# Hedgehog attention with a gated feed-forward: the product of the query exponentials with the key sums goes from VectorE to GpSimd

## The chip, the cores and the metric

The kernel runs on one core of one Trainium2 chip. The metric is device time in microseconds of that core, from runs of the whole program. A profiled execution, taken with the hardware profiler, shows what each engine did: TensorE does the matrix products (PE, with its weight loads as PEld), VectorE (DVE) and ScalarE (ACT) the element-wise work, GpSimd (POOL) element-wise work between buffers of the on-chip memory SBUF, and SyncE (SP) issues transfers. Only TensorE writes the accumulation memory PSUM in this kernel's products; VectorE and ScalarE read it.

## The reference

For 2048 rows of 576 features the reference computes a linear attention with a learned feature map, times a gate made by a feed-forward network, on the layer-normed input `xn`:

```python
pq = einsum("bhsd,hdf->bhsf", q, w_phi)          # 32 heads of 18
pk = einsum("bhsd,hdf->bhsf", k, w_phi)
phi_q = concat([softmax(pq), softmax(-pq)], -1)
phi_k = concat([softmax(pk), softmax(-pk)], -1)
kv  = einsum("bhsf,bhsd->bhfd", phi_k, v)
z   = einsum("bhsf->bhf", phi_k)
num = einsum("bhqf,bhfd->bhqd", phi_q, kv)
den = einsum("bhqf,bhf->bhq", phi_q, z)[..., None] + 1e-6
s   = (num / den) reshaped @ wo
g   = silu((silu(xn @ w_gate) * (xn @ w_up)) @ w_down)
out = x + s * g
```

What matters here is `den`: for each query row and head the 36 features are multiplied with the sums `z` over all keys, and added up.

## The kernel before

The program runs through four stages: layer norm with the transposed input and the folded weights; a key stage, which accumulates `kv` and `z`; a query stage, from about 218 to 457 us of the profiled execution; and the feed-forward, which fills the rest. Float32 products are made of three products of high and low parts, so TensorE has far more work than the plain sizes say.

The query stage handles sixteen tiles of 128 rows, two to a pair, in eight pairs. For a tile, `q_tile` makes the logits in the PSUM tile `p2` (28 products; there is one buffer of `p2`, so the next tile's logits have to wait until VectorE has read these), then `softmax_parts` takes maxima and minima (`m`, L530), subtracts them (`e`, L531, two halves), has ScalarE take the exponentials (L534, two halves) and VectorE add them up per head (`sm`, L538). Then come the lines around the change: `ez` is the product of the exponentials with `zb`, which holds the key sums `z` on all 128 partitions (L832); `y` is the sum of `ez` per head (L834); six small operations make the factor of each head (L836 to L841); and L842 multiplies the exponentials with it, `e<-e,y`. `numer` transposes the finished `e` of both tiles of a pair (`pt`, L854), splits them in high and low parts (`ph` by ScalarE L73, `pl` by VectorE L74), multiplies with `kv` (L861) and splits the result (`oh`, `ol`); `project` multiplies with `wo` (`p`, L889, 56 products). In program order the numerator of one pair comes ahead of the logits of the next.

Three other pieces of work run inside this stage. Early feed-forward tiles (`early_tile`, products `pe` at L108) need nothing of the attention and fill TensorE where it would wait. `tails` prepares pieces of the feed-forward weights: SP loads `tl` (L808), GpSimd makes four differences (L810 to L813), ScalarE and VectorE split them (`th` L815, `tl` L816), and GpSimd issues twelve transfers to `t_dram` (L819). `split_wo` splits `wo` in the first pair.

The order on each engine is fixed when the program is built. A planner in the language's library goes through all instructions, takes on each engine the one that comes first in program order among those that it holds to be ready, with its own estimate of how long each takes, and writes one list per engine; `issue_after` and `high_priority` shift a few places. On the chip every engine works through its list strictly in order, and waits at an instruction whose inputs are not there. So a filler product stands where the planner expected a gap, and what the planner estimated wrongly becomes a wait on the chip.

Of the kernel before, what the change touches and what calls it, by code (L numbers as in the profile page):

```python
# [52 lines left out]
def heads(ap):  # L53
    return ap.rearrange("p (h d) -> p h d", d=DH)


def spread(ap, n):
    return ap.unsqueeze(2).to_broadcast([P, n, DH])
# [3 lines left out]
def gated_hedgehog_kernel(ctx: ExitStack, tc, x, w_qk, w_v, consts_in, wo, w_gu, w_tail, w_down, out):  # L62
# [5 lines left out]
    nc = tc.nc  # L68
# [26 lines left out]
    def block(t):  # L95
        return t // HT, (t % HT) // 4, slice((t % 4) * P, (t % 4 + 1) * P)

    def xw(ps, i, j, cols, wh, wl, stationary_x):
        pairs = []
        for k in range(2):  # L100
            b = XB[i][2 * j + k]
            for c in range(2):
                pairs += [(b[:, c, cols], w[:, k, c]) for w in (wh, wl)]
                pairs += [(b[:, 3 + c, cols], wh[:, k, c])]
            pairs += [(b[:, 2, cols], wh[:, k, 2])]
        for n, (a, b) in enumerate(pairs):
            l, r = (a, b) if stationary_x else (b, a)
            last = nc.tensor.matmul(ps, l, r, start=n == 0, stop=n == len(pairs) - 1)  # L108
        return last
# [46 lines left out]
    with ExitStack() as att:  # L156
# [18 lines left out]
        with ExitStack() as wst:  # L175
# [349 lines left out]
            def softmax_parts(ps, e):  # L525
                m = kk_pool.tile([P, 2, H], F32, name="m", bufs=1)
                p4 = ps[:, :, 0:HALF].rearrange("p a (h d) -> p a h d", d=DH)
                for s, op in enumerate((ALU.max, ALU.min)):
                    m3 = m[:, s].rearrange("p (a h) -> p a h", a=2)
                    nc.vector.tensor_reduce(m3, p4, axis=AX.X, op=op)  # L530
                    read.append(nc.vector.tensor_sub(e[:, s * D:(s + 1) * D].rearrange("p (a h d) -> p a h d", a=2, d=DH),  # L531
                                                     p4, m3.unsqueeze(3).to_broadcast([P, 2, H // 2, DH])))
                for s in range(2):
                    last = nc.scalar.activation(e[:, s * D:(s + 1) * D], e[:, s * D:(s + 1) * D], AF.Exp,  # L534
                                                scale=1.0 if s == 0 else -1.0)
                exps.append(last)
                sm = kk_pool.tile([P, 2 * H], F32, name="sm")
                nc.vector.reduce_sum(sm, heads(e), axis=AX.X)  # L538
                return sm
# [206 lines left out]
        with ExitStack():  # L746
# [3 lines left out]
            zb = qc.tile([P, 2 * D], F32, name="zb")  # L750
# [33 lines left out]
        with ExitStack() as qst:  # L784
# [38 lines left out]
            def q_tile(t):  # L823
                i0, j0, cols = block(t)
                pq = qps.tile([P, 2, 512], F32, name="p2")
                for i in range(2):
                    w = slice(i * HALF, (i + 1) * HALF)
                    xw(pq[:, i, 0:HALF], i0, j0, cols, QH[:, :, :, w], QL[:, :, :, w], True)
                e = qk.tile([P, 2 * D], F32, name="e", bufs=4)
                r = softmax_parts(pq, e).rearrange("p (s h) -> p s h", s=2)  # L830
                ez = qk.tile([P, 2 * D], F32, name="ez", bufs=1)
                nc.vector.tensor_mul(ez, e, zb)  # L832
                y = qk.tile([P, 2 * H], F32, name="y")
                nc.vector.reduce_sum(y, heads(ez), axis=AX.X)  # L834
                y2 = y.rearrange("p (s h) -> p s h", s=2)
                nc.vector.scalar_tensor_tensor(y2[:, 0], r[:, 0], DEN_EPS, y2[:, 0], op0=ALU.mult, op1=ALU.add)  # L836
                nc.vector.tensor_mul(y2, y2, r[:, ::-1])
                den = qk.tile([P, H], F32, name="den")
                nc.vector.tensor_add(den, y2[:, 0], y2[:, 1])
                nc.vector.reciprocal(den, den)  # L840
                nc.vector.tensor_mul(y2, r[:, ::-1], den.unsqueeze(1).to_broadcast([P, 2, H]))  # L841
                last_e.append(nc.vector.tensor_mul(heads(e), heads(e), spread(y, 2 * H)))  # L842
                return e
# [56 lines left out]
            for n in range(S // QS + 1):  # L900
                new = []
                if n > 0:
                    om = numer(es)
                if n < S // QS:
                    new += [q_tile(order[n] * (QS // P) + j) for j in range(QS // P)]
                if n == 0:
                    split_wo()
                if n > 0:
                    project(order[n - 1], *om, n == S // QS)
                es = new  # L910
# [646 lines left out]
```

## Time and profile before

| | |
|---|---|
| median of three runs | 1579.47 us (1579.38 to 1579.89) |
| the profiled execution: its time | 1580.98 us |
| its span, first to last instruction | 1579.2 us |
| TensorE busy | 1570.4 us (99%) |
| VectorE busy | 1162.8 us (74%) |
| GpSimd busy | 671.5 us (43%) |
| granted TensorE clock | 1.00 |

The profiled execution took 1.5 us more than the median of the runs, and 1.8 us of its time lie outside the span. Sums over the trace are made against the span; a difference found there carries over to the time. Shares over the whole span mix stages with different limits: in the query stage VectorE is busy for 16 to 20 us of each 20 us, far above its mean.

### The profile page before, as it was taken

Reading aid. Unit: us, or ns where it says so; the run is one execution under the profiler, and the core shown is the slowest. Engines: PE = TensorE matmul, PEld = TensorE weight load, DVE = VectorE, ACT = ScalarE, POOL = GpSimd, SP = SyncE. Lnnn points to the kernel's source line nnn. Section 1 sums busy time; section 2 is a strip of 40 time slices with the busy share of each in tenths; the row PEclk is TensorE's granted clock in tenths of the full one; section 3 lists DMA queues with packets and bytes.
Section 4 is the critical chain, followed back from the end, with each engine's and each line's share of the span. In section 5 each row is a group of like instructions: output and inputs, shape, how many; then the busy total and the mean of one; then the engine's idle time right before and its main releaser. Section 6 shows DMA issues by size and latency. Waiting matters only on the chain.

```text
span 1579.2 us, 25305 instructions
## 1 busy us (share of the span) xinstructions
PE 1570.4 (99%) x9371; PEld 1415.5 (90%) x9371; DVE 1162.8 (74%) x1722; ACT 729.0 (46%) x1408; POOL 671.5 (43%) x723
## 2 busy tenths in 40 slices
PE   9999999999999999999999999999999999999998
PEld 7999999999988898898888888888888888888887
DVE  7777769999947787987777778545766667666577
ACT  6633344545445644444544444454333343333334
POOL 5766653334125545563644444313323324133133
PEclk9999999999999999999999999999999999999999
DMA  9424343336357455454545543964545655555445
GB/s 284 142 67 165 135 154 117 105 118 209 120 185 259 159 181 198 161 182 174 186 161 202 177 168 125 355 210 139 155 146 157 193 173 161 175 184 187 145 118 182
DMA packets 123287, 269.05 MB, mean 170 GB/s; under 512 B 12436, under 2 KB 54100, under 8 KB 121884
## 3 DMA queue, kind: packets, MB, share of 16 engines
q1 hardware_dynamic: 110572, 246.57, 47.6%
q0 software_dynamic: 3552, 12.59, 2.8%
q10 hardware_dynamic: 9040, 8.28, 1.6%
q8 instruction: 74, 1.21, 0.3%
q14 instruction: 49, 0.40, 0.1%
HBM read 167.54 MB, written 99.09 MB: 169 GB/s over the span
## 4 chain that ended last, share of the span: by engine, by line
PE 96%; POOL 1%; DVE 1%; DMA 1%; issue 1%; ACT 0%; SPq 0%; DVEq 0%; POOLq 0%; ACTq 0%
PE px L1014 25%; PE pd L1136 25%; PE pw L1014 12%; PE p L108 6%; PE py L1014 6%; PE pe L108 5%; PE p L889 4%; PE kvp L547 2%; PE pt L861 2%; PE pe L50 1%; PE vx L636 1%; PE pt L854 1%; PE tp L50 1%; PE vw L636 1%; DMA wst<-in_A_w_qk 0%
## 5 line engine op out<-in xcount | busy, mean ns | idle before, releaser
L1136 PEld LDWEIGHTS pd<-dw,hh 128*128 128x128 f32 x3000 | 421.8, 188 | 19.8 <-DVE acc L1372 0.8
L1136 PE MATMUL pd<-dw,hh 128*128 128x288 f32 x3000 | 435.7, 294 | 0.0
L1014 PE MATMUL px<-X,w 128*128 128x512 f32 x1512 | 385.6, 390 | 0.0
L1014 PEld LDWEIGHTS px<-X,w 128*128 128x128 f32 x1512 | 274.6, 188 | 46.1
L1014 PE MATMUL pw<-X,w 128*128 128x512 f32 x744 | 188.8, 389 | 0.0
L1014 PEld LDWEIGHTS pw<-X,w 128*128 128x128 f32 x744 | 139.5, 188 | 28.9
L1372 DVE TENSOR_TENSOR acc<-pd,acc 128x576 f32<-128x576 f32 x128 | 96.4, 753 | 93.3 <-PE pd L1136 92.6
L1047 DVE TENSOR_TENSOR s<-pw,s 128x512 f32<-128x512 f32 x126 | 86.4, 687 | 89.5 <-ACT s L1042 78.9
L1042 ACT COPY s<-px 128x512 f32<-128x512 f32 x126 | 73.6, 584 | 144.9 <-PE px L1014 144.7
L73 ACT CAST hh<-ha 128x512 fp32r<-128x512 f32 x139 | 82.2, 620 | 94.2 <-PE pd L1136 68.7
L74 DVE TENSOR_TENSOR hh<-ha,hh 128x512 fp32r<-128x512 f32 x139 | 111.8, 829 | 18.8 <-ACT hh L73 18.5
L1344 POOL TENSOR_TENSOR hb<-hb 128x512 f32<-128x512 f32 x34 | 46.6, 1372 | 157.2 <-DVE hb L1059 156.8
L74 DVE TENSOR_TENSOR w<-ld,w 128x512 fp32r<-128x512 f32 (+1 forms) x96 | 76.9, 803 | 38.6 <-ACT w L73 37.7
L1014 PE MATMUL px<-X,wt 128*128 128x512 f32 x252 | 98.0, 389 | 0.0
L1014 PE MATMUL py<-X,w 128*128 128x512 f32 x378 | 96.5, 390 | 0.0
L1357 POOL TENSOR_TENSOR ha<-ha 128x512 f32<-128x512 f32 x34 | 52.3, 1554 | 100.1 <-DVE hh L74 94.7
L1331 POOL TENSOR_TENSOR h<-ha,hb 128x512 f32<-128x512 f32 x34 | 44.5, 1309 | 107.2 <-DVE ha L1063 76.4
L983 POOL TENSOR_TENSOR ts<-ld 128x256 f32<-128x256 f32 x32 | 26.8, 839 | 139.6 <-issue 67.4
L73 ACT CAST w<-ld 128x512 fp32r<-128x512 f32 (+1 forms) x96 | 52.7, 550 | 70.3 <-POOL ld L986 40.6
L1067 ACT COPY py<-px 128x512 f32<-128x512 f32 x63 | 36.0, 572 | 106.1 <-PE px L1014 94.6
L108 PE MATMUL pe<-X,wh 128*128 128x512 f32 x260 | 80.4, 395 | 0.0
L1014 PEld LDWEIGHTS py<-X,w 128*128 128x128 f32 x378 | 68.3, 188 | 10.8
(325 smaller groups left out, 3242.3 us busy)
## 6 DMA issues: line engine op xcount, KB each, us to landing
w_dram<-w SPq DMA_DIRECT2D x90, 512.0 KB, 2.6
w<-w_dram SPq DMA_DIRECT2D x90, 512.0 KB, 4.3
wt<-t_dram SPq DMA_DIRECT2D x62, 336.0 KB, 4.4
ld<-in_B_w_gu SPq DMA_DIRECT2D x32, 512.0 KB, 6.3
rt<-in_B_w_down SPq DMA_DIRECT2D x33, 288.0 KB, 5.1
rb<-in_B_w_down SPq DMA_DIRECT2D x33, 288.0 KB, 3.3
w_dram<-w SPq DMA_DIRECT2D x30, 256.0 KB, 2.1
w<-w_dram SPq DMA_DIRECT2D x30, 256.0 KB, 2.7
```

The costliest lines, as they stand in the source:

```text
L73: cast = nc.scalar.copy(hi, src)
L74: return cast, nc.vector.tensor_sub(lo, src, hi)
L108: last = nc.tensor.matmul(ps, l, r, start=n == 0, stop=n == len(pairs) - 1)
L889: nc.tensor.matmul(ps[:, 0:HALF], a, bw, start=k == 0, stop=k == len(mm) - 1)
L1014: nc.tensor.matmul(ps, l, r, start=first and n == 0, stop=last and n == len(mm) - 1, skip_group_check=True)
L1042: snaps.append(nc.scalar.copy(t, ps))
L1047: nc.vector.tensor_add(t, ps, t)
L1136: nc.tensor.matmul(ps, l, r, start=first and n == 0 and m == 0, stop=n == len(hs) - 1 and m == 2, skip_group_check=True)
L1331: sub(s, g["h"][0][0], g["h"][0][1])
L1344: nc.gpsimd.tensor_add(a21, a21, g["h"][1][1])
L1357: sub(a12, a12, g["h"][0][0])
L1372: adds.append(nc.vector.tensor_add(a2, pd[:, :, 0:HALF], a2))
```

## The change

In `q_tile`, the product of the exponentials with the key sums is issued to GpSimd instead of VectorE. Nothing else in the source differs:

```diff
                 e = qk.tile([P, 2 * D], F32, name="e", bufs=4)
                 r = softmax_parts(pq, e).rearrange("p (s h) -> p s h", s=2)
                 ez = qk.tile([P, 2 * D], F32, name="ez", bufs=1)
-                nc.vector.tensor_mul(ez, e, zb)
+                nc.gpsimd.tensor_mul(ez, e, zb)
                 y = qk.tile([P, 2 * H], F32, name="y")
                 nc.vector.reduce_sum(y, heads(ez), axis=AX.X)
```

The planner makes a new order from it. The instructions are the same apart from the sixteen that change engine, and the lists of all engines agree up to the query stage and, but for a few transfers and differences at its end, from the feed-forward on. In between they differ at three places that matter here.

GpSimd, at the start of the query stage, behind the last split of the key stage's sums (`slo`). Before:

```order
L580 TENSOR_TENSOR slo<-sraw,shi 128x512
L810 TENSOR_TENSOR tl<-tl 128x128
L811 TENSOR_TENSOR tl<-tl 128x128
L812 TENSOR_TENSOR tl<-tl 128x128
L813 TENSOR_TENSOR tl<-tl 128x128
L810 TENSOR_TENSOR tl<-tl 128x128
```

and with the change:

```order
L580 TENSOR_TENSOR slo<-sraw,shi 128x512
L810 TENSOR_TENSOR tl<-tl 128x128
L832 TENSOR_TENSOR ez<-e,zb 128x1152
L811 TENSOR_TENSOR tl<-tl 128x128
L812 TENSOR_TENSOR tl<-tl 128x128
L810 TENSOR_TENSOR tl<-tl 128x128
L813 TENSOR_TENSOR tl<-tl 128x128
```

The first tile's `ez` stands behind the first difference of the tail weights, L810, which needs the load of `tl`.

VectorE, the first tile and the logits of the second (`p_2505`). Before:

```order
L538 TENSOR_REDUCE sm<-e 128x64
L832 TENSOR_TENSOR ez<-e,zb 128x1152
L530 TENSOR_REDUCE m<-p_2505 128x32
L834 TENSOR_REDUCE y<-ez 128x64
L531 TENSOR_TENSOR e<-p_2505,m 128x576
L836 SCALAR_TENSOR_TENSOR y<-sm,y 128x32
L530 TENSOR_REDUCE m<-p_2505 128x32
L837 TENSOR_TENSOR y<-y,sm 128x64
L531 TENSOR_TENSOR e<-p_2505,m 128x576
```

and with the change:

```order
L538 TENSOR_REDUCE sm<-e 128x64
L834 TENSOR_REDUCE y<-ez 128x64
L530 TENSOR_REDUCE m<-p_2505 128x32
L836 SCALAR_TENSOR_TENSOR y<-sm,y 128x32
L531 TENSOR_TENSOR e<-p_2505,m 128x576
L837 TENSOR_TENSOR y<-y,sm 128x64
L530 TENSOR_REDUCE m<-p_2505 128x32
L839 TENSOR_TENSOR den<-y 128x32
L531 TENSOR_TENSOR e<-p_2505,m 128x576
```

`y` now stands directly behind `sm`, ahead of all reading of the second tile's logits.

VectorE, the fourth tile (its last read of the logits stands some rows ahead). Before:

```order
L531 TENSOR_TENSOR e<-p_2704,m 128x576
L816 TENSOR_TENSOR tl<-tl,th 128x896
L538 TENSOR_REDUCE sm<-e 128x64
L832 TENSOR_TENSOR ez<-e,zb 128x1152
L834 TENSOR_REDUCE y<-ez 128x64
L836 SCALAR_TENSOR_TENSOR y<-sm,y 128x32
```

and with the change:

```order
L842 TENSOR_TENSOR e<-e,y 128x1152
L74 TENSOR_TENSOR ol<-pt,oh 126x256
L538 TENSOR_REDUCE sm<-e 128x64
L834 TENSOR_REDUCE y<-ez 128x64
L816 TENSOR_TENSOR tl<-tl,th 128x896
L836 SCALAR_TENSOR_TENSOR y<-sm,y 128x32
```

Here too `y` follows `sm` at once, and L816, the low part of the first tail weights, stands behind it. Over the sixteen tiles `y` stands directly behind `sm` in ten; in the other six, one or two short operations lie between. On TensorE the filler products between the starts of the first and the seventh pair's projections go from 169 to 108, and stand behind the last projection instead.

## The prediction

> **What bounds the kernel now.** I read the page's busy times and its chain of waits first, then the busy times in stretches of the query stage, then the groups of that stage, then single instructions around two of its tiles.
>
> ```profile
> PE 1570.4 (99%) x9371; PEld 1415.5 (90%) x9371; DVE 1162.8 (74%) x1722; ACT 729.0 (46%) x1408; POOL 671.5 (43%) x723
> PE 96%; POOL 1%; DVE 1%; DMA 1%; issue 1%; ACT 0%; SPq 0%; DVEq 0%; POOLq 0%; ACTq 0%
> ...
> 240.00:260.00 20.00, 20.00 (x112) 17.28 (x111) 19.91 (x32) 10.81 (x17) 2.41 (x6) 1.00 0.38 120
> 280.00:300.00 20.00, 20.00 (x149) 19.47 (x149) 18.89 (x31) 10.11 (x19) 5.69 (x13) 1.00 0.31 86
> 360.00:380.00 20.00, 20.00 (x144) 18.97 (x142) 19.29 (x31) 10.61 (x19) 6.48 (x13) 1.00 0.76 251
> ...
> 456.98 10.89 PE pe L108 x48
> ```
>
> TensorE is busy 99% of the span, and the chain that ended last runs through it for 96%. In the query stage (the stretches from 240 on; the columns are PE, PEld, DVE, ACT, POOL) it is never idle, but VectorE stands at 19 to 20 of 20 us beside it: here two engines are at their limit, and the fillers `pe` are what keeps TensorE full. One filler product costs 10.89/48 = 0.227 us. The number of products does not change, so the time can only change by what TensorE waits. It waits for next to nothing now, so there is next to nothing to gain.
>
> How tightly the two are coupled shows at the sixth tile, in the order of time:
>
> ```profile
> 301.08 1.52 DVE L842 TENSOR_TENSOR e<-e,y 128x1152 f32<-128x1152 f32 x1
> ...
> 302.27 0.40 PE L108 MATMUL pe<-X,wh 128*128 128x512 f32 x1
> 302.65 0.85 PE L854 MATMUL pt<-consts,e 128*72 128x128 f32 x6
> ```
>
> L842 ends at 302.60, and the transposes start 0.05 us later: the planner placed as many fillers as VectorE's chain took, to within one product. If that chain is later on the chip than the planner thinks, TensorE stands still for all of the difference.
>
> **What moves, and its price.** From the groups of the query stage, and of GpSimd over the whole span:
>
> ```profile
> L842 DVE TENSOR_TENSOR e<-e,y 128x1152 f32<-128x1152 f32 x16 | 22.0, 1374 | 0.4
> L832 DVE TENSOR_TENSOR ez<-e,zb 128x1152 f32<-128x1152 f32 x16 | 21.6, 1350 | 0.0
> L538 DVE TENSOR_REDUCE sm<-e 128x64 f32<-128x1152 f32 x16 | 21.6, 1347 | 1.6 <-ACT e L534 1.4
> L834 DVE TENSOR_REDUCE y<-ez 128x64 f32<-128x1152 f32 x16 | 21.5, 1346 | 0.1
> ...
> L1413 POOL TENSOR_TENSOR acc<-acc,X 128x1152 f32<-128x1152 f32 x2 | 6.3, 3133 | 8.3 <-DVE acc L1372 8.3
> L1407 POOL TENSOR_TENSOR X<-X,acc 128x1152 f32<-128x1152 f32 x2 | 5.3, 2672 | 13.6 <-DVE sx L1406 12.3 <-PE pw L1014 1.4
> ```
>
> VectorE loses sixteen times 1.35 us, 21.6 us. GpSimd has done the same form (two inputs, 128x1152, float32) in 2.67 and 3.13 us, so it gets sixteen times that, 43 to 50 us. I take 2.67, since `sm`, which has one input, is what runs beside it on VectorE. `ez` can start with `sm`, as both need only the exponentials. So where VectorE did `sm` and `ez` in 2.70 us, `y` can now start 2.67 us plus a handover of about 0.1 us after the exponentials: the chain of one tile is no shorter, but VectorE stands idle for 1.4 us of it, unless it has something else in its list there.
>
> **Term 1, the first tile.** Its `ez` stands in GpSimd's list behind L810, which needs the load of `tl`. What the trace has there:
>
> ```profile
> L808 SPq DMA_DIRECT2D tl<-in_B_w_tail x2: 357/394/430, 228.3 to 228.7; - x2
> DMA to landing us min/median/max: 6.7/6.7/6.7
> ...
> 226.06 1.26 ACT L534 ACTIVATE e<-e 128x576 f32<-128x576 f32 x2
> 229.35 1.35 DVE L538 TENSOR_REDUCE sm<-e 128x64 f32<-128x1152 f32 x1
> 232.56 1.34 DVE L834 TENSOR_REDUCE y<-ez 128x64 f32<-128x1152 f32 x1
> 235.17 0.47 POOL L810 TENSOR_TENSOR tl<-tl 128x128 f32<-128x128 f32 x1 [9.64 <-DMA h_dram<-h]
> 235.64 0.74 DVE L531 TENSOR_TENSOR e<-p,m 128x576 f32<-128x576 f32 x1
> 235.71 0.46 POOL L811 TENSOR_TENSOR tl<-tl 128x128 f32<-128x128 f32 x1
> 236.53 0.37 PE L108 MATMUL p<-QH,X 128*128 128x288 f32 x1
> ```
>
> The load is issued at 228.3 and lands 6.7 us later, at 235.0; L810 starts at 235.17, after GpSimd has waited 9.64 us. Everything ahead of this place is unchanged, so the load lands then again. The exponentials are ready at 227.3, but `ez` cannot start before L811 did, at 235.7. It ends at 235.7 + 2.67 = 238.4, and `y` starts at 238.5 instead of 232.56. Behind `y` on VectorE waits the reading of the second tile's logits (the second `e` L531, before at 235.64 to 236.38, 3.8 us after `y` started). In the new order one more `m` (0.7 us) and one small operation lie between, so it ends at 238.5 + 3.8 + 0.9 = 243.2. For that read waits TensorE: `p2` has one buffer, and the third tile's logits, at 236.53 before, start at 243.3. Its list now has five fillers fewer ahead of them (21 for 26), so it is there at 236.3 - 5 x 0.227 = 235.1, and stands still for 8.2 us. The chain behind it (L842 of the first tile, and the second tile's sixteen later VectorE operations) costs some 0.9 us more at the two transposes, and 0.6 us of waiting there before falls away. Term 1 is 8.5 us. Its ends are 8.0, if the later transposes come in time, and 9.5 with 3.13 us for `ez`.
>
> **Term 2, the other tiles.** In nine of the fourteen tiles from the third on, `y` stands directly behind `sm`, and waits 2.67 + 0.1 - 1.35 = 1.4 us: 12.8 us. In the other five one or two splits lie between (0.42 or 0.68 us each, 0.7 to 1.4 us in all), and 2.0 us are left. So VectorE waits 14.8 us in these tiles. Whether TensorE does depends on whether the planner counted this wait when it placed fillers. At the fourth tile it put L816, 1.08 us of work that nothing late holds up, behind `y`: it held `y` to be ready when `sm` ended. And it took 169 - 108 = 61 fillers out of six pairs, 61 x 0.227 = 13.8 us, close to the 6 x 2.7 = 16.2 us that VectorE is relieved of there, as if nothing came back. So most of the wait reaches TensorE. Some is taken up where VectorE waits anyway, for ScalarE's half of the splits:
>
> ```profile
> L74 DVE TENSOR_TENSOR pl<-pt,ph 126x512 fp32r<-126x512 f32 (+1 forms) x40 | 26.3, 685 | 6.1 <-ACT ph L73 5.9
> L74 DVE TENSOR_TENSOR ol<-pt,oh 126x256 fp32r<-126x256 f32 x32 | 13.2, 420 | 4.4 <-ACT oh L73 4.3
> ```
>
> That is 10.2 us in eight pairs; I let half of it, 5 us, cover the wait. Term 2 is 10 us. Its ends are 0 (the planner counted right) and, with 3.13 us in fourteen tiles and no cover, 14.8 + 14 x 0.46 = 21 us.
>
> GpSimd may also be held up by VectorE:
>
> ```profile
> 237.31 1.50 DVE L842 TENSOR_TENSOR e<-e,y 128x1152 f32<-128x1152 f32 x1
> 237.68 1.45 POOL L811 TENSOR_TENSOR tl<-tl 128x128 f32<-128x128 f32 x1
> ```
>
> L811 took 0.46 us alone at 235.71, and 1.45 beside L842, until that ended. In five pairs L842 of the first tile runs just when `ez` of the second becomes ready; but `sm` stands behind that same L842, so `y` is later by the 1.4 us above either way, and I add nothing. The Trainium skill states the rule behind it (GPSIMD Engine Reference, 8. Key points): GpSimd shares its SBUF interfaces with VectorE and contends with VectorE instructions that read two SBUF inputs. `sm` and `y` read one, so by this rule too they leave `ez` alone, and the term stays 10 us.
>
> **The sum.** 8.5 + 10 = 18.5 us on a span of 1579.2 us: 1597.7, and with the 1.8 us around it 1599.5 us for such an execution. That one lay 1.5 us above the median of the runs, so for the median 1579.5 + 18.5 = 1598 us. Behind the last projection the fillers that moved keep TensorE full, and the feed-forward's order is as before; I count nothing there.
>
> **The rivals.**
>
> *The first tile alone.* The planner's estimate of GpSimd is right, and only the landing surprises it: 1579.5 + 8.5 = 1588 us. Against it speaks L816's place. 20%.
>
> *GpSimd's list holds `ez` up all along.* Between the products stand eight blocks of twelve transfer issues, some of which wait for ScalarE or VectorE:
>
> ```profile
> L819 POOL DMA_DIRECT2D t_dram<-th x64 | 31.5, 499 | 53.6 <-ACT th L815 30.2 <-ACT so L895 22.4 <-issue 0.2
> ```
>
> If in half of the pairs one `ez` stands behind eight issues, that is 4 x 8 x 0.5 = 16 us more, 1614 us. For it speaks that term 1 is just such a case; against it, that behind the first pair most issues end well before the next exponentials. 12%.
>
> *TensorE keeps pace: not slower.* VectorE, relieved of 21.6 us in the one stage where it is full, runs ahead of TensorE, so that `y`'s waits fall into its own idle time, and the first logits are not held. Then TensorE only saves what it waited for in that stage, about 1 us: 1578.5 us. It would decide if `tl` landed by 229, some 6 us sooner. Nothing that precedes the load has changed, so I give it 6%.
>
> *A slower array after the long stop.* The first products of the program show what a cold start costs:
>
> ```profile
> L169 PE MATMUL fp<-idle x25: 379/379/634, 1.0 to 8.1; 128*128 128x512 bf16 x25
> ```
>
> The last of 25 starts 7.1 us after the first, 24 intervals, where 24 x 0.227 would be 5.4: 1.7 us lost, with the slowest at 634 ns for 379. If 8 us of standing still bring that back, the time is 1600 us; I hold it for one in two, and as 1600 lies within the forecast's own range, it takes nothing from the other chances. The Trainium skill (TensorE: Matmul & The Clock Gate, The two states you'll see) says that the clock falls to half after an idle window of about 3.4 us and comes back after as long a busy one. By that rule the stop of 8.2 us is long enough; no row of this trace has a stop like it in mid-program.
>
> **How the numbers follow.** The forecast, 1598 us, has 62%; its own range is 1591 to 1606. The first tile alone has 20%, GpSimd's list 12%, not slower 6%. The range for 8 in 10 reaches from 1587 (term 1 at its lower end, term 2 nothing) to 1609 (9.5 + 21). About 0.2%, 3.2 us, is what a measurement of this kernel can tell from no change. Slower than that are the first three, 94%; of the last 6% I give 4 to within 0.2% and 2 to faster, since TensorE has so little waiting to save.
>
> **What would show it.** In the changed profile: L810 at about 235.2 and the first `ez` directly behind it; the first L834 on VectorE with some 7 us of idle time ahead of it, put down to GpSimd's `ez`; a stop of TensorE of about 8 us before the third tile's logits, near 243; `ez` at 2.7 us; waits of about 1.4 us before most other L834; TensorE idle before L854 in most pairs, for L842, 1 to 2 us each. It would be wrong if the first L834 starts before 235, if TensorE's stops lie elsewhere (then the list or the transfers are at fault), or if the waits before L834 come without stops on TensorE.

## The result, and the profile after

The changed kernel takes 1606.67 us (median of four runs, 1605.65 to 1608.18), the kernel before 1579.68 us (1579.38 to 1583.2) beside it: a ratio of 1.0166, 95% interval 1.0149 to 1.0184. The change makes it slower by 27.0 us. The profiled executions differ by a little less, 25.0 us: 1605.96 us for 1580.98, with spans of 1604.2 and 1579.2 us.

The page of the changed kernel, busy times and the chain that ended last:

```profile
PE 1575.5 (98%) x9371; PEld 1416.4 (88%) x9371; DVE 1143.4 (71%) x1706; ACT 723.9 (45%) x1404; POOL 709.6 (44%) x739
PE 86%; POOL 4%; DVE 4%; issue 2%; ACT 2%; DMA 1%; SPq 0%; POOLq 0%; ACTq 0%; DVEq 0%
...
L832 POOL TENSOR_TENSOR ez<-e,zb 128x1152 f32<-128x1152 f32 x16 | 45.0, 2815 | 90.6 <-ACT e L534 90.6
```

VectorE is busy for 19.4 us less; 21.6 us of products left it, but other instructions became longer, L78 alone by 1.6 us in the query stage. But TensorE's share of the chain falls from 96% to 86%: GpSimd, VectorE and ScalarE have come into it. The last row says that where GpSimd stood idle ahead of `ez`, it was the exponentials of ScalarE that ended the wait; this holds for fifteen of the sixteen products, and the first one has no idle time, as it follows L810 at once.

Where the time went shows in what TensorE waited for from 216 to 490 us (us in total, times, longest). In the kernel before this view has one row:

```profile
PE pt L854 <- DVE e L842: 0.2, 1, 0.2
```

In the changed kernel:

```profile
PE pt L854 <- DVE e L842: 10.0, 8, 1.7
PE p L108 <- DVE e L531: 7.3, 1, 7.3
PE pt L861 <- DVE pl L74: 2.5, 3, 1.4
PE p L889 <- ACT so L895: 0.5, 1, 0.5
PE pt L854 <- DVE ol L74: 0.4, 1, 0.4
PE p L889 <- DVE ol L74: 0.3, 1, 0.3
```

21.0 us for 0.2. The 7.3 us is one stop, at the first pair; this is its course in the timeline (start, duration, instruction, idle time ahead of it and what ended that):

```profile
233.54 0.46 POOL L810 TENSOR_TENSOR tl<-tl 128x128 f32<-128x128 f32 x1 [9.41 <-DMA h_dram<-h]
233.96 2.61 POOL L832 TENSOR_TENSOR ez<-e,zb 128x1152 f32<-128x1152 f32 x1
236.60 1.35 DVE L834 TENSOR_REDUCE y<-ez 128x64 f32<-128x1152 f32 x1 [7.29 <-POOL ez L832]
240.35 0.76 DVE L531 TENSOR_TENSOR e<-p,m 128x576 f32<-128x576 f32 x1
241.25 0.58 PE L108 MATMUL p<-QH,X 128*128 128x288 f32 x1 [7.33 <-DVE e L531]
```

The load of `tl` lands, GpSimd makes one difference and only then the product, VectorE adds it up, reads the second tile's logits, and TensorE may write the third tile's. (The row of L810 names another transfer, `h_dram`, which was issued 0.9 us behind the load; in the source L810 reads nothing but `tl`, and E4 below, where L810 waits too, has the load in its row.) The other tiles show in the group of `y`:

```profile
L834 DVE TENSOR_REDUCE y<-ez 128x64 f32<-128x1152 f32 x16 | 21.7, 1353 | 21.8 <-POOL ez L832 21.6
```

21.6 us of waiting for `ez`, 7.3 of it in the first tile, 14.3 in the others; before, the same group had 0.1 us.

The stop also cost the clock. The columns are the stretch and its length, the busy time of TensorE, its weight loads, VectorE, ScalarE and GpSimd, and then the granted clock, DMA share and GB/s:

```profile
230.57:233.98 3.41, 3.35 (x15) 2.44 (x13) 0.00 (x0) 0.00 (x0) 0.44 (x2) 1.00 1.05 334
233.98:237.39 3.41, 0.00 (x0) 0.00 (x0) 0.79 (x1) 0.00 (x0) 3.41 (x5) 1.00 0.45 179
237.39:240.80 3.41, 0.00 (x0) 0.00 (x0) 3.41 (x8) 1.34 (x2) 2.10 (x5) 0.50 0.00 0
240.80:244.22 3.42, 2.97 (x12) 3.00 (x13) 2.31 (x5) 3.38 (x5) 0.11 (x1) 0.50 0.00 0
244.22:247.63 3.41, 3.41 (x25) 3.22 (x24) 3.40 (x3) 3.39 (x5) 2.57 (x1) 1.00 0.02 5
```

After the stop twelve products of the logits took 2.97 us at half clock, where twelve take 1.6 us (0.132 us each from start to start): 1.4 us lost. So the first tile costs 7.3 + 1.4 = 8.7 us.

### The profile page after: what moved, and what is told of

It reads as the page before. It is cut to its first block, busy times and chain, and to the rows that moved or that the text cites. A ratio compares the mean times of both kernels' runs of the same rounds, so it can differ in the third digit from the quotient of the medians.

```text
span 1604.2 us, 25320 instructions
## 1 busy us (share of the span) xinstructions
PE 1575.5 (98%) x9371; PEld 1416.4 (88%) x9371; DVE 1143.4 (71%) x1706; ACT 723.9 (45%) x1404; POOL 709.6 (44%) x739
## 4 chain that ended last, share of the span: by engine, by line
PE 86%; POOL 4%; DVE 4%; issue 2%; ACT 2%; DMA 1%; SPq 0%; POOLq 0%; ACTq 0%; DVEq 0%
PE px L1014 25%; PE pd L1136 25%; PE pw L1014 12%; PE py L1014 6%; PE p L108 4%; PE pe L108 3%; POOL ez L832 2%; PE kvp L547 2%; PE pe L50 1%; PE vx L636 1%; PE pt L861 1%; PE tp L50 1%; PE pt L854 1%; PE p L889 1%; DVE y L834 1%
## 5 line engine op out<-in xcount | busy, mean ns | idle before, releaser
L832 POOL TENSOR_TENSOR ez<-e,zb 128x1152 f32<-128x1152 f32 x16 | 45.0, 2815 | 90.6 <-ACT e L534 90.6
```

Of the source, the lines that this page charges most:

```text
L832: nc.gpsimd.tensor_mul(ez, e, zb)
```

## The experiments

The theory that went into the runs: both terms are waits for GpSimd, 8.7 us at the first tile and some 16 us at the others. The rivals: the first tile alone; GpSimd's work as such, which could slow VectorE or ScalarE, whoever waits for it; or the planner's new order. The kernel before took 1580.1 to 1580.2 us beside these runs.

**E1, only the first tile's `y` waits.**

```diff
-                nc.vector.reduce_sum(y, heads(ez), axis=AX.X)
+                nc.vector.reduce_sum(y, heads(e if last_e else ez), axis=AX.X)
```

> Only the first tile's `y` reads `ez`; the other fifteen read `e`, so that they wait for nothing on GpSimd. GpSimd still makes all sixteen products, in the same place of the same list (the key sums are left out of fifteen tiles' denominators). My theory, two terms: the first tile costs 7.5 us of TensorE standing still plus 1.2 us at half clock = 8.7 us, and the other tiles' waits cost the remaining 16 us. So this kernel should take 1579.7 + 8.7 = 1588.4 us, between 1586 and 1591, with `y` waiting 7.3 us for `ez` once and never again. Rival, the work itself: GpSimd's products slow VectorE and ScalarE down, or their order is worse, whoever waits for them; then it stays near 1604. Rival, the first tile is nearly everything: 1600 or more.

(`last_e` is empty in the first tile, so here the condition is true from the second tile on.) Measured: 1594.4 us, ratio 1.0090 (1.0076 to 1.0103). `y` waited once, for 7.1 us. The lists of all engines are those of the changed kernel, so the waits of the other tiles cost 12.3 us. But 6 us more than my first-tile term stay.

**E2, no `y` waits.**

```diff
-                nc.vector.reduce_sum(y, heads(ez), axis=AX.X)
+                nc.vector.reduce_sum(y, heads(e), axis=AX.X)
```

> All sixteen `y` read `e`, none reads `ez`; GpSimd still makes all products, and TensorE and GpSimd have the same lists as in the changed kernel (the key sums are left out of all denominators). My theory: both terms are waits for GpSimd; with nobody waiting, VectorE has 21.6 us less to do than before and TensorE is not held: 1579.7 us or up to 3 us less, 1577 to 1581. Rival, GpSimd's work as such costs time (it holds up VectorE or ScalarE, or its transfers to `t_dram` come late): more than 1584, and up to 1606 if that is all of it.

Measured: 1589.6 us, ratio 1.0059 (1.0046 to 1.0071). My theory missed by 9 us. One reason is in its waits:

```profile
PE pt L854 <- DVE e L842: 4.5, 2, 4.0
DVE e L842 <- POOL ez L832: 3.8, 1, 3.8
```

L842 writes `e` in place, so it must wait until GpSimd has read `e`. Where `ez` is late by the load of `tl`, the wait moves from `y` to L842 and TensorE still stands for some 4 us, at the first transposes, long enough for 3.4 us at half clock. To get rid of the first tile's stop, `ez` itself has to come sooner.

**E3, the first tile's product on VectorE, the other fifteen on GpSimd.**

```diff
-                nc.gpsimd.tensor_mul(ez, e, zb)
+                (nc.gpsimd if last_e else nc.vector).tensor_mul(ez, e, zb)
```

> The first tile's `ez` is made by VectorE as before the change, the other fifteen by GpSimd; the same result is computed. My theory: term 1 (8.7 us) is gone and term 2 (about 16 us) stays: 1606.7 - 8.7 = 1598 us, between 1594 and 1601. Rival, the first tile alone makes the difference: 1580 to 1582. Rival, the place of L810 is not the cause and the wait only moves to the second tile: 1604 or more.

Measured: 1601.3 us, ratio 1.0132 (1.0118 to 1.0146): 5.4 us gained, just above the range that I expected, and 20 us above the rival "first tile alone". The planner made another order here, on TensorE too (`y` waits 15.4 us in all), so the single terms are better read from E5.

**E4, half of each product on either engine.**

```diff
-                nc.gpsimd.tensor_mul(ez, e, zb)
+                nc.gpsimd.tensor_mul(ez[:, 0:D], e[:, 0:D], zb[:, 0:D])
+                nc.vector.tensor_mul(ez[:, D:2 * D], e[:, D:2 * D], zb[:, D:2 * D])
```

> Each tile's product is made in two halves of 576 columns at the same time, the first on GpSimd, the second on VectorE; the same result is computed. A half on GpSimd should take 1.35 us and one on VectorE 0.7, so that from the third tile on `y` waits for no more than about 0.1 to 0.6 us where it waited 1.4. Yet each half reads two inputs, and if GpSimd stands still while VectorE's half runs, as it did beside L842, its half ends 2.0 us after the start, and `y` is ready 0.6 us later than with VectorE alone. My theory: term 1 stays (8.7 us), term 2 falls from 16 to between 0 and 7: 1588 to 1596, 1592 taken. Rival, any wait for GpSimd costs the same however short: 1604 or more. Rival, the gain of halving VectorE's work shows: 1586 or less.

Measured: 1586.6 us, ratio 1.0041 (1.0027 to 1.0055), better than I expected: here the planner put the first `ez` ahead of the differences (it starts at 226.7), so term 1 fell away too, and no `y` waits for GpSimd. It is still 6.5 us slower than leaving the whole product on VectorE.

**E5, `ez` ahead of the tail's differences in GpSimd's list.** All other rows of all lists are those of the changed kernel (two lines more, so `y` is L836, L842 is L844, `th` L816).

```diff
-                nc.gpsimd.tensor_mul(ez, e, zb)
+                ezs.append(nc.gpsimd.tensor_mul(ez, e, zb))
...
-                sub(t[:, 4], t[:, 2], t[:, 0])
+                with tc.issue_after(ezs[0].ins):
+                    sub(t[:, 4], t[:, 2], t[:, 0])
...
```

> The four differences of the tail weights stand behind the first tile's `ez` in GpSimd's list; every other row of every list is as in the changed kernel, and the same result is computed. My theory: the first tile's stop of TensorE (7.5 us) and the half clock behind it (1.2 us) are gone, the other tiles' waits stay: 1606.7 - 8.7 = 1598 us, between 1596 and 1600. Rival, the differences are now late themselves, and `tl` L816 or the transfers to `t_dram` hold VectorE or `ez` up: 1602 or more. Rival, GpSimd is not the cause of the stop: 1606.

Measured: 1601.8 us, ratio 1.0138 (1.0124 to 1.0151): 4.8 us gained, not 8.7. The stop of 7.3 us is gone, but another of 1.9 us stands in its place, with half clock behind it (3.4 us of it, with TensorE full: 1.7 us lost). What is late now is VectorE. The timelines of VectorE and GpSimd in E5:

```profile
226.56 3.75 DVE L78 TENSOR_TENSOR wl<-raw,wh 128x512 fp32r<-128x512 f32 x2
226.69 3.07 POOL L834 TENSOR_TENSOR ez<-e,zb 128x1152 f32<-128x1152 f32 x1 [1.91 <-ACT e L534]
...
236.91 0.37 PE L108 MATMUL p<-QH,X 128*128 128x288 f32 x1 [1.87 <-DVE e L531]
```

and VectorE's same two instructions in the changed kernel, where `ez` was not yet running:

```profile
225.88 1.28 DVE L78 TENSOR_TENSOR wl<-raw,wh 128x512 fp32r<-128x512 f32 x2
```

Two splits that take 1.28 us took 3.75. They end 0.55 us after `ez` does (226.69 + 3.07 = 229.76, 226.56 + 3.75 = 230.31): the first took its usual 0.68 us, the second 3.15 us. I read this as the second having to wait until GpSimd was done, which E10 tests; everything behind it on VectorE is 2.5 us late.

**E6, nobody waits and `ez` is ahead:** the edits of E2 and E5 together.

> Both at once: `ez` of the first tile ahead of the differences, and all `y` read `e` (the key sums are left out of the denominators), so that neither `y` nor the in-place L842, which must let GpSimd finish reading `e`, waits for GpSimd. TensorE has the list of the changed kernel. With the wait of `y` alone taken away 1589.6 us were left; 4.1 us of that was the stop before the first transposes, where L842 waited for GpSimd's reading of `e`, and some 1.5 us the half clock behind it. My theory: the remaining 4 us are small stops that the changed order itself has (fewer feed-forward products between the attention's): 1584 us, between 1582.5 and 1585.5. Rival, no cost is left once nobody waits for GpSimd: 1578 to 1581.

Measured: 1589.2 us, ratio 1.0059 (1.0045 to 1.0073). All engines have the lists of E5. It differs from E5 by the waits of the other tiles' `y`, 14.3 us, and by 12.6 us of time: nearly all of a wait on VectorE in this stage reaches the end. But 9 us above the kernel before are left where I expected 4. The stop at the third tile's logits (2.2 us) and the half clock behind it are still there, as L78 is kept out here too. The other stops that have a name are not in the order, as I held, but behind a third effect: TensorE waits 1.9 us for `pl`, and in E10, with the same lists, none of that is left. ScalarE's group of `th`, before and in E6:

```profile
L815 ACT CAST th<-tl 128x896 fp32r<-128x896 f32 x8 | 7.5, 943 | 2.5 <-ACT so L895 2.3 <-ACT e L534 0.2
```
```profile
L816 ACT CAST th<-tl 128x896 fp32r<-128x896 f32 x8 | 7.5, 943 | 13.0 <-POOL tl L814 10.3 <-DVE y L843 2.2 <-ACT e L534 0.5
```

and one such place in E6's timelines of GpSimd, ScalarE, VectorE and TensorE:

```profile
337.09 2.67 POOL L834 TENSOR_TENSOR ez<-e,zb 128x1152 f32<-128x1152 f32 x1 [5.34 <-ACT e L534]
341.75 0.46 POOL L814 TENSOR_TENSOR tl<-tl 128x128 f32<-128x128 f32 x1
342.24 0.94 ACT L816 CAST th<-tl 128x896 fp32r<-128x896 f32 x1 [1.87 <-POOL tl L814]
343.09 0.37 ACT L73 CAST oh<-pt 126x256 fp32r<-126x256 f32 x1
343.49 0.42 DVE L74 TENSOR_TENSOR ol<-pt,oh 126x256 fp32r<-126x256 f32 x1 [1.36 <-ACT oh L73]
343.97 0.69 DVE L74 TENSOR_TENSOR pl<-pt,ph 126x512 fp32r<-126x512 f32 x1
344.72 0.50 PE L863 MATMUL pt<-ph,KVH 126*126 126x256 f32 x2 [1.10 <-DVE pl L74]
```

GpSimd's product puts off the four differences behind it, ScalarE waits for the last of them at `th`, the split of `pt` queued behind it comes late, and with it VectorE's half and TensorE.

**E7, `y` after both tiles' exponentials** (with E5's edit): `q_tile` returns after `ez`, and the rest, from `y` on, stands in a function that is called for both tiles of the pair afterwards.

```diff
-                    new += [q_tile(order[n] * (QS // P) + j) for j in range(QS // P)]
+                    new += [weigh(*a) for a in [q_tile(order[n] * (QS // P) + j) for j in range(QS // P)]]
```

> As the run with `ez` ahead of the differences, and `y` and all that follows it in a tile is emitted for both tiles of a pair only after both tiles' logits and exponentials, so that the reading of the second tile's logits comes first where both are ready; the same result is computed. In six of the first tiles of a pair other work (splits, the second tile's first reading) now lies between `sm` and `y`; in most of the second tiles `y` still follows `sm` directly. My theory: the wait counts where nothing lies between; half of the 12 us of the other tiles' waits is hidden, but `y` is also later in the second tile: 1598 - 6 = 1592 us, between 1586 and 1596. Rival, GpSimd is too slow wherever `y` stands: 1597 or more.

Measured: 1598.7 us, ratio 1.0120 (1.0106 to 1.0133); a miss, and what the rival had said. `y` still waits 11.0 us in ten tiles: VectorE's lists leave less between `sm` and `y` than I had counted. Against E5 the waits fell by 3.3 us and the time by 3.1.

**E8, as E7, with only the first tile of each pair on GpSimd.**

```diff
-                ezs.append(nc.gpsimd.tensor_mul(ez, e, zb))
+                ezs.append((nc.gpsimd if t % 2 == 0 else nc.vector).tensor_mul(ez, e, zb))
```

> As the last one, but only the first tile of each pair has its `ez` on GpSimd, the second on VectorE; the same result is computed. Now each product on GpSimd has VectorE's reading of the second tile's logits beside it, and no `y` of a second tile waits. My theory: no more than 1 us of waits is left, and VectorE has 10.8 us less to do than before, which TensorE, which stood still for some 5 us in the stage before, can use in part: 1578 us, between 1576 and 1583. Rival, the planner again leaves too few feed-forward products where the waits are, and stops of 4 us or more stay: 1584 or more.

Measured: 1587.3 us, ratio 1.0045 (1.0032 to 1.0057); a miss, and within the rival's 1584 or more. The waits of `y` are down to 2.3 us, but 7 us stay. TensorE again stands 2.0 us at the third tile's logits, with half clock for 3.4 us behind it: L78 is kept out by the first `ez`, as in E5.

**E9, no product at all.**

```diff
-                ez = qk.tile([P, 2 * D], F32, name="ez", bufs=1)
-                nc.gpsimd.tensor_mul(ez, e, zb)
...
-                nc.vector.reduce_sum(y, heads(ez), axis=AX.X)
+                nc.vector.reduce_sum(y, heads(e), axis=AX.X)
```

> No engine makes the product: the sixteen `ez` are gone and `y` reads `e` (the key sums are left out of the denominators). VectorE has 21.6 us less to do than before, and GpSimd nothing more. It tells whether the small stops of TensorE that stay when nobody waits for GpSimd (0.5 to 1.3 us each, 3.7 us together) come from the order, in which the planner leaves fewer feed-forward products between the attention's because it holds VectorE to be less busy. If so, they stay without any work on GpSimd: 1583.5 us, between 1582 and 1586, slower than before though there is less to do. Rival, they come from GpSimd's work beside VectorE's: 1577 to 1580.5.

Measured: 1582.8 us, ratio 1.0017 (1.0008 to 1.0026). With 21.6 us of VectorE's work dropped the kernel is 2.8 us slower than before (1.3 to 4.1 by the interval). GpSimd does nothing more here, so what is lost belongs to the order that the planner makes when it holds VectorE to be relieved. It is an order of its own: from about 300 us on its lists differ from those of the changed kernel, so these 2.8 us are not the price of the changed kernel's order. In this run TensorE has only two named waits of 1.1 us together in the stage, so the small stops of E6 are not in this order; the value fits what I expected, the reason does not. Where all of the 2.8 us lie is not settled.

**E10, GpSimd copies instead of multiplying.** TensorE, VectorE and ScalarE have E6's lists.

```diff
-                ezs.append(nc.gpsimd.tensor_mul(ez, e, zb))
+                ezs.append(nc.gpsimd.tensor_copy(ez, e))
```

> As the run in which nobody waits and `ez` is ahead of the differences, but GpSimd copies `e` (one input) where it multiplied (two inputs); TensorE, VectorE and ScalarE have the same lists as in that run (the key sums are left out of the denominators). There VectorE's second `wl` L78, which reads two inputs, took 3.15 us where 0.68 is usual, and ended 0.55 us after GpSimd's product did; TensorE stood still for 2.4 us at the third tile's logits, and the clock was half for 3.4 us. My theory: GpSimd's two-input product keeps VectorE's two-input instruction out until it has ended; a copy does not, or is over sooner. Then L78 takes under 1.5 us, the stop is under 1 us, the clock stays, and the time is 1589.2 - 2 - 1.7 = 1585.5 us, between 1584 and 1587. Rival, any GpSimd instruction of that size keeps VectorE out as long, and the time stays at 1589; rival, L78 is long for another reason (its inputs), and stays at 3.15 us with GpSimd's copy long over.

Measured: 1584.3 us, ratio 1.0025 (1.0016 to 1.0035): 4.9 us less than E6 with the same lists. GpSimd and VectorE at the first tile, and the group of `th`:

```profile
226.09 1.57 POOL L834 COPY ez<-e 128x1152 f32<-128x1152 f32 x1 [1.86 <-ACT e L534]
225.97 2.23 DVE L78 TENSOR_TENSOR wl<-raw,wh 128x512 fp32r<-128x512 f32 x2
...
L816 ACT CAST th<-tl 128x896 fp32r<-128x896 f32 x8 | 7.5, 942 | 5.5 <-POOL tl L814 2.4 <-DMA t_dram<-tl 1.8 <-DVE tl L817 0.8
```

The copy keeps VectorE out just as the product did (the splits again end 0.54 us after it), only for a shorter time. The stop at the logits falls to 0.8 us, the clock stays, and ScalarE waits 2.4 us for differences where it waited 10.3. So the late L78 and the late differences are both set by how long GpSimd's instruction takes. The 4.9 us are about 1.4 of the stop (2.2 to 0.8), 1.7 of the clock and 1.9 of TensorE's waits for `pl`.

**E11, as E8 without E5's edit, and the first pair's products on VectorE.**

```diff
-                ezs.append((nc.gpsimd if t % 2 == 0 else nc.vector).tensor_mul(ez, e, zb))
+                ezs.append((nc.gpsimd if t % 2 == 0 and len(ezs) > 1 else nc.vector).tensor_mul(ez, e, zb))
```

> As the run with only the first tile of each pair on GpSimd and a later `y` (1587.3 us), but the first pair's `ez` are both on VectorE, so that seven products are on GpSimd; the same result is computed. My theory: of that run's 7 us above the kernel before, 2.1 us were the stop at the third tile's logits (L78 kept out by `ez`) and 1.7 us the half clock behind it; both go: 1583.5 us, between 1581 and 1585.5, with the clock at full speed in the whole stage. Rival, the order costs the rest wherever the first product is: 1586 or more. Rival, all losses were at the first tile: 1580 or less, a version as fast as the kernel before or faster.

Measured: 1585.8 us, ratio 1.0036 (1.0023 to 1.0050), just above my range: the stop at the third tile's logits and the half clock are gone, but 1.5 us were gained and not 3.8; the lists are others than in E8, and what the rest of 5.7 us is no run shows. No variant with the product, or part of it, on GpSimd reaches the kernel before.

## Why the prediction was right, and where its sum was short

The prediction gave 1598 us with a range of 1587 to 1609 and 94% for slower; measured are 1606.7 us. The direction and both mechanisms held. The size was short: the sum was 18.5 us, and it came to 25.0 us in the spans and 27.0 in the medians. The time lies 0.7 us above 1591 to 1606, the range of the forecast itself. (The upper end of the wide range is a slip: 9.5 + 21 us give 1610, not 1609.) The runs cut the whole into pieces, each step from one run to the next:

```
changed kernel                             1606.7
ez ahead of the differences       (E5)     1601.8    -4.8
and nobody waits                  (E6)     1589.2   -12.6
and a copy for the product        (E10)    1584.3    -4.9
and nothing on GpSimd             (E9)     1582.8    -1.5
kernel before                              1580.1    -2.8
```

The first three steps are made on the same lists of all engines, but for the place or the kind of `ez` itself. The last two go through E9's own order, so only their sum, 4.2 us, belongs to the changed kernel's lists: E10 has 1.9 us of named waits of TensorE, and where its other 2.3 us lie is open. E9 makes it likely that they come from the order; it does not show it.

- **Term 1, the first tile: 8.5 us forecast, 8.7 us in the trace.** The chain ran as described, some two microseconds sooner throughout: L810 at 233.54, `ez` directly behind it, `y` at 236.60, TensorE again at 241.25. That the two figures agree is luck. The stop was 7.3 us for 8.2, the 0.9 us at the two transposes did not appear (no wait there in the trace), and 1.4 us of half clock, which the sum did not hold, made up for it. Of these 8.7 us only 4.8 come back when `ez` is moved ahead, since VectorE is then kept out of L78 by the running `ez`, and a second stop with its half clock takes its place (1.9 + 1.7 us).
- **Term 2, the other tiles: 10 us forecast.** The waits of `y` were right, 14.3 us for 14.8, and TensorE's stops stood where the prediction put them: eight before L854, 0.3 to 1.7 us each, 10.0 us together. The mis-sized step is the cover: I let 5 us of the waits be taken up by VectorE's waits for ScalarE. E5 and E6, with the same lists, show that 12.6 of the 14.3 us reach the end (12.3 by E1 against the changed kernel), so the cover was 1.7 us. VectorE's waits for `ph` and `oh` fit that: 7.4 and 5.5 us in E6, 6.0 and 5.2 in E5, so the later `y` took up 1.7 us of them. Why no more, no run shows.
- **What was not in the sum.** First, ScalarE's waits at `th` for GpSimd's differences, 6.7 us in the changed kernel, which cost TensorE some 1.9 us (the waits for `pl` in E6 that E10 does not have). I had looked at GpSimd waiting for `th`, not at `th` waiting for GpSimd. Second, the 2.3 us of E10 without a name, perhaps the order. Of the 6.5 us by which the sum was short in the spans, the missing cover is 2.6 us (12.6 for 10), these two are some 4; the pieces overlap, and I don't divide it further.
- **`ez` at 2.7 us, and no add-on for L842: right.** `ez` took 2.6 to 2.7 us where nothing stood beside it; the mean of 2.815 us comes from four that met L842 (2.9 to 3.6 us), and `y`, behind that same L842, waited no longer for them (1.3 us).
- **The rivals.** The first tile alone would have left E3 and E5 at 1580 to 1582 us; they take 1601 to 1602. GpSimd's list held `ez` up in the first tile only: in the other fifteen GpSimd stood idle ahead of `ez`, 90.6 us together, until the exponentials came. That TensorE keeps pace was wrong, and even E9, where nobody waits for GpSimd and VectorE is relieved, is not faster than before. The clock rival, which I held for one in two, came true, with 1.4 us for 1.7.
- **The contention was seen from one side.** The prediction weighed how VectorE holds up GpSimd and found nothing to add. What costs is the reverse: GpSimd's long instruction keeps VectorE out. In the changed kernel's first tile no such instruction met it (in the second one did: an L78 of 2.0 us), in E5, E6 and E8 one did.

## What to carry to other kernels

Where an engine works through its list in order and is nearly full beside the one that sets the time, a wait of 1 us on it can be worth nearly 1 us at the end (12.6 of 14.3 here), even if the work moved away is larger than the wait. Idle time that the engine had before is not cover by itself: of some 10 us, 1.7 served as such here. Before moving work to a slower engine, look at three things: what stands ahead of it in that engine's list (here one load), what stands behind it there and who waits for that (here ScalarE's `th`), and which instructions of the first engine the longer one will keep out. Where a planner sets the order, relieving an engine can cost time by itself: 2.8 us (1.3 to 4.1) with nothing put in its place.

## What the runs showed of the hardware

**A window of 3.41 us decides on TensorE's clock, and it need not be idle throughout.** In the query stage the clock stood at half for 3.41 us or twice that, never for another length. The windows follow one another without a break: from the rise of the clock at the start to its fall in the query stage it is 68 times 3.413 us in the changed kernel (5.28 to 237.39) and in E5, and 112 times in E7, so the windows below are counted in such steps. In E5 and E7 nearly the same stop, 1.9 and 2.2 us, had different ends. E5, then E7 (columns as above; TensorE's busy time is the third figure, the granted clock the third from the right):

```profile
234.32:237.73 3.41, 1.54 (x10) 1.11 (x9) 3.34 (x10) 2.49 (x3) 3.04 (x7) 1.00 0.49 197
237.73:241.15 3.42, 3.42 (x17) 3.36 (x16) 2.50 (x3) 3.39 (x5) 2.73 (x2) 0.50 0.00 0
```
```profile
231.82:235.24 3.42, 2.33 (x11) 1.59 (x9) 3.42 (x6) 0.69 (x2) 1.55 (x4) 1.00 1.01 367
235.24:238.65 3.41, 2.26 (x16) 2.14 (x16) 3.21 (x6) 3.37 (x4) 2.02 (x5) 1.00 0.05 20
238.65:242.06 3.41, 3.41 (x22) 3.14 (x22) 2.90 (x2) 3.41 (x5) 2.68 (x1) 1.00 0.02 5
```

In E5 the stop fell into one window, TensorE was busy for 1.54 of 3.41 us, and the next window ran at half clock. In E7 it fell across two, each with 2.3 us of work, and the clock stayed. (The fall of E7's clock is a later one, at 388.84, behind a window with 0.85 us of work.) The closest case on the other side is in E3:

```profile
344.19:347.60 3.41, 1.66 (x11) 1.18 (x10) 1.60 (x3) 1.48 (x3) 1.99 (x5) 1.00 0.00 0
347.60:351.01 3.41, 3.27 (x17) 2.79 (x18) 3.34 (x9) 1.27 (x2) 2.54 (x6) 1.00 0.66 162
```

1.66 us of work kept the clock. So in these runs the border lies between 1.54 and 1.66 us of work in a window, a little under half, and a full window at half clock costs 1.7 us. The Trainium skill (TensorE: Matmul & The Clock Gate, The two states you'll see) gives the same window and says that the clock falls after an idle one; the traces agree on the length, and show that a window with 45% of work in it is enough. A stop of 2 us can thus cost 3.7, or 2, by where it falls.

**GpSimd and VectorE can keep each other out until an instruction has ended.** VectorE's `wl` L78 (0.68 us), which reads two inputs in SBUF, waited until GpSimd's instruction had ended, whether that was a product with two inputs (E5: the pair of splits 3.75 us for 1.28) or a copy with one (E10: 2.23). The Trainium skill (GPSIMD Engine Reference, 8. Key points) says that the two contend; here it is no slowing down in part, but a wait of up to the other's full length, in both directions: in the changed kernel `ez`, 2.66 us by itself, took up to 3.58 where VectorE's L842 was running. VectorE's instructions with one input in SBUF were not kept out: `sm` took 1.35 us beside `ez` as without it, and `pl`, nearly of L78's shape (126x512) but with one of its inputs in PSUM, its usual 0.68.
